# Loading expert 2's two weight matrices earlier in a kernel of linear attention and eight dense experts

## The chip, the cores and the metric

The kernel runs on one core of a Trainium2 chip. A core has five engines that run their own instruction streams in order: TensorE (PE in the profile, with its weight loads as PEld), VectorE (DVE), ScalarE (ACT), GpSimd (POOL) and SyncE (SP). They meet through semaphores. Transfers between HBM and the on-chip memory run on 16 DMA engines; SP and POOL issue them, and each of the two has a queue of its own (queue 1 for SP's, queue 0 for POOL's in the profile). The metric is device time in microseconds of one execution. Less is better.

## The reference

The input is a linear attention with 8 batches, 8 heads, 576 positions and head dimension 64, followed by eight experts that every token passes, with weights from a Sinkhorn routing:

```python
q_p, k_p = (phi(q), phi(k))                      # phi(x) = elu(x) + 1
kv = np.einsum('bhsd,bhse->bhde', k_p, v)
z = np.sum(k_p, axis=2)
x = num / den                                    # q_p @ kv over q_p . z, laid out as (4608, 512)

P = np.exp(x @ w_gate - max)                     # (4608, 8)
for _ in range(8):
    P /= P.sum(1, keepdims=True) + 1e-09
    P /= P.sum(0, keepdims=True) + 1e-09
    P *= N / E
for e in range(E):                               # E = 8 experts, each on all 4608 tokens
    h = np.maximum(x @ w1[e], 0.0)               # w1[e]: 512 x 1024
    out += P[:, e:e + 1] * (h @ w2[e])           # w2[e]: 1024 x 512
```

Each expert has two weight matrices of half a million elements. The kernel holds them as 16-bit floats, so each is 1 MB on the chip. All eight experts must be computed for all tokens, so the weights are read once per expert, and the work is almost all matrix multiplication.

## The kernel before, in words

**Tiling.** The 4608 tokens are nine groups of 512, which the code calls units (`g` = 0 to 8). The attention runs first, and expert 0 is woven into it. Experts 1 to 7 then run one after another over the nine groups, in the order `SUBS = [(0,), (1, 2), (3, 4), (5, 6), (7, 8)]`: one single unit and four double units of two groups each. A double unit takes two steps (`q` = 0 and 1), each for half of the hidden width of both groups. A step `n` is the first layer of one such half (`l1_half`) beside the second layer of a group whose hidden values are ready (`layer2`, lines 1065 to 1187).

**Seven products for eight.** Both layers multiply 2 by 2 blocks with seven products. This needs sums of the operands: of the tokens (in HBM as the tensors `xd`, seven blocks per unit, written once by `x_blocks`), of the weights (`combos`: four sums W of w1, line 1038, and four sums T of w2, line 1052), and of the hidden values (four sums S, line 1083). These sums run on VectorE.

**Names of the products.** In a step the first layer's products are `a1` to `a7` and `b1` to `b7` (lines 816 and after), the second layer's are `y1` to `y7` (line 1112). The order of TensorE is written out by hand, the same for every step, where A1, A5, A6, A3 and A2 are the next step's a1, a5, a6, a3 and a2:

```python
order = "y1 y5 y2 a7 y6 y3 a4 b1 b5 y7 b6 b3 b2 b7 A1 A5 y4 b4 A6 A3 A2".split()
```

**x blocks.** `x_load` (line 781) has SP load the seven blocks of a unit in the order 1, 5, 6, 3, 2, 7, 4, each 256 KB for a double unit. There are ten buffers for them (tiles `xs`), seven until the token tile is given up. A load waits until TensorE has read the block that lay in its buffer. From then on SP issues them in batches of seven while TensorE is in the `b` products of a unit's second step: blocks 3, 2, 7 and 4 of the next unit, whose first step is about to begin (its A1 and A5 are among TensorE's next products), and then blocks 1, 5 and 6 of the unit after that. The first loads behind the token tile also wait for the end of the routing (`P_sb`, line 586).

**Weights.** `load_w` (line 308) has POOL issue the loads. w1 takes two DMA issues of 512 KB, w2 of experts 1 to 7 takes one of 1024 KB. There are two buffers for each of w1 and w2, so expert 2's w1 goes into the buffer of expert 0's, and expert 2's w2 into that of expert 0's w2. POOL also adds two pieces of each group's second layer into the sums (line 1153, tiles `acc`), for experts 1 to 7, after ScalarE has scaled them (`st`, line 1150); the groups' tiles are acc_87 (group 0), acc_88 (group 1), acc_89, and so on.

**Planner.** No instruction is issued while `add(...)` runs. Each `add` hands a task to `_Plan`, with its engine, its assumed cost, the tasks that it depends on (`deps`) and its priority. `_Plan.run` then simulates the engines and emits the tasks in the order that comes out. For the front part, up to somewhat into expert 1's and expert 2's work, this order is not left to the simulation: the string `_FRONT` lists tasks by number and engine letter (g is POOL, m a DMA, s SP, n none), and `run` emits in exactly that order. It insists that each task is allowed at its place, which means that its `deps` are done and its buffer is free in the simulation. The hardware's semaphore waits come only from the data: who wrote or read a buffer last. `deps` of the planner set places in the order and add no wait of their own.

Tasks 1513, 1514 and 1515 are the buffer, the POOL issues and the DMA of expert 2's w1; tasks 1516, 1517 and 1518 are those of its w2.

Of the kernel before, what the change touches and what calls it, by code (L numbers as in the profile page):

```python
# [181 lines left out]
543d 1025p 986p 1029p 941a 937a 1026a 932d 944p 1030a 1031p 1027p 1028a 1033p 987a 544d 938p 545p 1034d 1035p 1037p 1036a 1038a 1032d  # L182
945d 1039p 1040a 546d 547d 933d 946p 1043p 1044a 1045p 1041p 1047p 1065p 548p 549d 550d 1046d 947a 988p 942p 1000n 1057s 1058m 943d
1059s 1060m 1048d 1042a 1061s 1062m 1063s 1064m 1066a 989p 996a 1147s 1148m 1149s 1150m 1067p 1068a 990p 1049p 1071p 1050a 1072a 1151s 1152m
728d 1005d 1006d 629a 1121d 991p 997a 992p 892a 1073p 994p 1122d 1007d 1069p 1123d 1074d 1070a 625a 1075p 627d 697a 993p 1076d 1077p
691d 1079p 1081p 664a 1080a 631d 1008d 1082a 1078a 995p 1085p 1086a 1087p 1083p 1089p 1093p 1095p 1124d 999d 1090d 1088d 998d 1091p 1084a
1094a 1513n 1099p 1096a 939d 1101p 1097p 1125p 1127p 1128d 695d 1092a 1100a 1129d 1126a 1130p 1131a 1103p 1135p 1138p 1104d 1105p 1107p 1136d
1098a 775d 1139d 1137d 662a 1109p 1141p 1106a 1108a 1113p 1516n 1153s 1154m 1155s 1156m 1110a 1115p 1114a 1133a 730a 1132g 1134g 1157s 1158m
1111p 1102d 1117p 1161p 1163p 1112a 1142d 1140d 1116d 1143d 1144p 1118d 1119p 1159s 1160m 1269s 1270m 1271s 1272m 1273s 1274m 1162a 1167p 1164a
658a 1120a 1169p 1168a 1165p 1146d 1145d 1189d 1190d 1193p 1195p 1194a 1198p 1171p 1203p 1166a 660a 1191d 1192d 1197d 726d 1196d 1201a 1202g  # L190
1199a 1206p 1172d 1173p 1174a 1175p 1176a 1177p 1178a 1205d 1204d 1209p 1181p 1182a 1183p 1179p 724d 1185p 1207d 1170d 1211d 1208d 1210d 1186d
1215p 693a 1217p 1212p 1187p 1243d 1200g 1514g 1515m 1244d 1214d 777d 1213d 1245d 774d 1246d 1180a 1216a 1221p 832a 1218a 1223p 1219p 1247p
1249p 1222a 1250d 1224d 1251d 1220a 1248a 1252p 1255a 1256g 951a 1188a 1225p 1226d 1184d 1257p 1259d 1260p 1258d 1519d 893d 1261d 1227p 1228a
1229p 1230a 1231p 1232a 833a 1263p 1235p 1237p 1275s 1276m 1233p 1236a 1239p 1253a 1264d 1520d 1521d 1265d 1277s 1278m 1279s 1280m 1281s 1282m
1283p 1391s 1392m 1393s 1394m 1285p 1266p 1240d 1234a 1284a 1238d 1241p 1289p 1286a 1291p 1287p 1395s 1396m 1242a 835a 1268d 1262d 1267d 1315p
1290a 1316a 1311d 1317p 1320p 1312d 1313d 1321a 1319d 1318d 1314d 1293p 1325p 1328p 776d 1294d 1295p 1288a 1327d 1330d 1326d 1329d 1297p 1299p
1331p 1296a 1298a 1303p 1292d 1300a 1305p 1301p 1332d 1365d 1333d 1304a 1307p 1337p 1339p 1334p 1366d 1302a 1517g 1518m 1254g 1308d 1309p 1323a
1338a 891a 1335d 1336d 1343p 1340a 1345p 1341p 1322g 950d 1369p 1371p 1344a 1342a 1370a 1374p 1347p 1379p 1346d 1522d 1367d 1373d 1368d 1372d
1382p 1377a 1310a 1378g 1324g 1348d 1349p 1351p 1352a 1380d 1306d 948d 1353p 1354a 1381d 1384d 1385p 1386d 1357p 1359p 1355p 1387d 1350a 1358a
1361p 1405p 1356a 1375a 1376g 1406a 1407p 1388p 1397s 1398m 1399s 1400m 1401s 1402m 1403s 1404m 1527s 1528m 1529s 1530m 1531s 1532m 1533s 1534m  # L200
# [21 lines left out]
def kernel(  # L222
# [85 lines left out]
    def load_w(ten, nm, pl, pieces, e, prio, deps=(), shape=None):  # L308
        g = S_.grp(pl)
        ts_ = []  # L310

        def f_al(_):
            g["tile"] = wpool.tile(shape, FP16, tag=nm, name=nm)
        tal = add(("none", 0.0), f_al, acq=[g], prio=prio, deps=deps)
        for part in pieces:
            def fn(_, part=part):
                for sl, off, ap in part:
                    nc.gpsimd.dma_start(out=g["tile"][sl], in_=AP(tensor=ten.tensor, offset=e * DM * F + off, ap=ap))
            gsw = [S_.grp(p_sw) for _ in part]
            ti = add(("pool", 0.8 * len(part)), fn, acq=gsw, use=[g, *gsw], prio=prio, deps=[tal, w_part.get(nm) if ts_ else None],  # L320
                     after=1.75)
            w_part[nm] = ti
            ts_.append(add(("dma", len(part) * (1.55 if len(part) * len(pieces) > 2 else 2.7)), lambda _: None, deps=[ti],
                           use=[g, *gsw], prio=prio, lat=2.15))
        return g, [ts_[0], ts_[-1]]

    def load_w1(e, parts=1, **kw):
        if parts > 1:
            return load_w(moe_w1, "w1", p_w1, [[((slice(64 * r, 64 * r + 64), slice(2 * i, 2 * i + 2)),
                                                 256 * F * r + 2 * PW * F * i, [[F, PW], [PW * F, 2], [1, F]]) for r in range(2)]  # L330
                                               for i in range(2)], e, shape=[P, NDT, F], **kw)
        return load_w(moe_w1, "w1", p_w1, [[((slice(64 * r, 64 * r + 64),), 256 * F * r, [[F, PW], [PW * F, NDT], [1, F]])
                                            for r in range(2)]], e, shape=[P, NDT, F], **kw)

    def load_w2(e, parts=1, **kw):
        n = NFT // parts
        return load_w(moe_w2, "w2", p_w2, [[((slice(None), slice(n * i, n * i + n)), n * i * P * DM,
                                             [[DM, P], [DM * P, n], [1, DM]])] for i in range(parts)], e,
                      shape=[P, NFT, DM], **kw)
# [284 lines left out]
    w_t = {0: load_w1(0, prio=-290.0, parts=2)}  # L624
# [151 lines left out]

    xst_of, xse_done, sx_users = {}, [], []

    n_load, first_x = [0], []

    def x_load(d, prio):
        gx = {}
# [135 lines left out]
    def l1_half(e, d, q, n, st):  # L918
        gw1, tw1 = w_t[e][:2]
        gW, tW = st["W"]  # L920
        un = NG + n
        dbl = len(SUBS[d]) == 2
        if q == 0:
            st["x"] = x_load(d, un)
            if n == 1:
                first_x.extend(t for _, t, _ in st["x"].values())
        gx = st["x"]
        r0, r1 = sorted((h_free.pop(0), h_free.pop(0)))
        slots = {0: (r0, r1)} if dbl else {0: (r0,), 1: (r1,)}
        if dbl:  # L930
            for s, r in enumerate((r0, r1)):
                st["h"].setdefault(SUBS[d][s], {})[q] = r
        else:
            st["h"][SUBS[d][0]] = {0: r0, 1: r1}
        blk = {i: gx[i][2] for i in ORD}
        for m in range(2):
            gi = 2 * q + m if dbl else m

            def F(i, p, gi=gi):
                return 2 * (gi if dbl else 2 * gi + p) + i - 1  # L940

            def A(i, j, F=F):
                return lambda p, c: gw1["tile"][:, 2 * (j - 1) + c, ts(F(i, p), P)]

            def W(i, gi=gi):
                return lambda p, c: gW["tile"][:, i - 1, c, gi if dbl else 2 * gi + p, :]

            def dst(fh, t, m=m):
                if dbl:
                    k = 2 * m + fh  # L950
                    a, b = 4 * r0 + k, 4 * r1 + k
                    return hb[:, a:b + 1:b - a, 256 * t:256 * t + 256]
                a = 4 * (r0, r1)[m] + fh
                return hb[:, a:a + 3:2, 256 * t:256 * t + 256]
            nm = {}
            rows = (r0, r1) if dbl else ((r0, r1)[m],)
            th = []
            pair(e, un, m, nm, 1 if dbl else 2, A, W, blk, dst, tw1, tW, [gw1, gW],
                 {i: ([gx[i][0]], [gx[i][1]]) for i in ORD}, th, [t for r in rows for t in h_users[r]],
                 n == 0, sx_users)  # L960
            for i, t in nm.items():
                pe_id[(n, f"{'ab'[m]}{i}")] = t
            pe_id[(n, "ab"[m] + "22")] = th[2]
            for s, g in enumerate(SUBS[d]):
                st["th"].setdefault(g, {0: [], 1: []})[q if dbl else m].extend(th)
# [288 lines left out]
    def second(n):  # L1254
        e, g = pend.pop(0)
        st = state[e]
        rows = st["h"][g]

        def H(j):
            return hb[:, 4 * rows[j]:4 * rows[j] + 4]  # L1260
        if not pend and n > len(steps):
            return last(g, NG + n, H, st["th"][g])
        own = layer2(e, g, NG + n - 1, H, st["th"][g], *st["T"], [])
        for j in range(2):
            h_users[rows[j]] = own
            h_free.append(rows[j])
        return None
    for n, (e, d, q) in enumerate(steps):
        if e not in state:
            if e >= 2:  # L1270
                w_t[e] = load_w1(e, prio=float(e), deps=w_t[e - 1][1][1:] + (first_x if e == 2 else [])) + load_w2(e, prio=float(e), deps=w_t[e - 1][3][1:])
            co = combos(e)
            state[e] = {"W": co[0:2], "T": co[2:4], "h": {}, "th": {}}
        l1_half(e, d, q, n, state[e])
        if n >= 2:
            second(n)
        if q == len(SUBS[d]) - 1:
            pend.extend((e, g) for g in SUBS[d])
# [10 lines left out]
    n = len(steps)  # L1289
# [38 lines left out]
```

## Time and profile before

| what | us |
|---|---|
| median of 3 runs | 961.14 |
| lowest and highest run | 959.94, 962.22 |
| the profiled execution, its own time | 963.2 |
| its span, from the first to the last instruction | 961.4 |
| TensorE busy in the span | 948.1 |
| VectorE busy in the span | 776.4 |
| ScalarE busy in the span | 582.8 |
| GpSimd busy in the span | 143.4 |

All places in time are microseconds from the span's start. Lines such as L1112 are lines of the kernel before. A row of the timeline gives the start, the length, the engine, the line, the operation, what it writes and reads, the shape and how many it stands for; in square brackets stands how long the engine had been idle ahead of it, and for what it waited. A matmul's row ends somewhat after the next one starts, since matmuls overlap; TensorE's pace is read from the starts. The granted clock is the share of its full clock that TensorE was given.

### The profile page before, as it was taken

Reading aid. Unit: us, or ns where it says so; the run is one execution under the profiler, and the core shown is the slowest. Engines: PE = TensorE matmul, PEld = TensorE weight load, DVE = VectorE, ACT = ScalarE, POOL = GpSimd, SP = SyncE. Lnnn points to the kernel's source line nnn. Section 1 sums busy time; section 2 is a strip of 40 time slices with the busy share of each in tenths; the row PEclk is TensorE's granted clock in tenths of the full one; section 3 lists DMA queues with packets and bytes.
Section 4 is the critical chain, followed back from the end, with each engine's and each line's share of the span. In section 5 each row is a group of like instructions: output and inputs, shape, how many; then the busy total and the mean of one; then the engine's idle time right before and its main releaser. Section 6 shows DMA issues by size and latency. Waiting matters only on the chain.

```text
span 961.4 us, 18327 instructions
## 1 busy us (share of the span) xinstructions
PE 948.1 (99%) x7008; PEld 652.8 (68%) x7008; DVE 776.4 (81%) x1500; ACT 582.8 (61%) x1033; POOL 143.4 (15%) x209
## 2 busy tenths in 40 slices
PE   8999999998999999999999999999999999999997
PEld 4565588665677666766667666766667666776665
DVE  7899999976888888878887888878887888877775
ACT  7899766765665555555555555555555555555551
POOL 6442000010111111111112111111112111111110
PEclk9999999998999999999999999999999999999999
DMA  9998863236226222642226422542226522215544
GB/s 242 255 247 190 198 159 105 78 91 151 77 68 131 83 77 78 148 105 76 71 72 141 105 78 77 125 97 74 73 74 154 119 78 77 72 45 164 165 133 132
DMA packets 81508, 112.65 MB, mean 117 GB/s; under 512 B 7436, under 2 KB 45196, under 8 KB 81420
## 3 DMA queue, kind: packets, MB, share of 16 engines
q1 hardware_dynamic: 56844, 75.65, 25.6%
q0 software_dynamic: 23856, 34.78, 19.3%
q8 instruction: 55, 0.90, 0.4%
q10 hardware_dynamic: 720, 1.05, 0.3%
q14 instruction: 33, 0.27, 0.1%
HBM read 119.69 MB, written 17.69 MB: 143 GB/s over the span
## 4 chain that ended last, share of the span: by engine, by line
PE 95%; DVE 2%; ACT 1%; DMA 1%; issue 0%; DVEq 0%
PE ye L1112 36%; PE hq L816 24%; PE R L816 12%; PE Zye L1112 6%; PE Zye L816 6%; PE ye L996 3%; PE hq L701 3%; PE yw L603 1%; PE kv_ps L427 1%; DMA xs<-xd 1%; PE att L484 1%; PE num_ps L484 1%; PE att L453 1%; PE hq L1208 0%; PE att L529 0%
## 5 line engine op out<-in xcount | busy, mean ns | idle before, releaser
L1143 DVE SCALAR_TENSOR_TENSOR acc<-ye,P_sb,acc 128x256 f32<-128x256 f32 x620 | 268.2, 479 | 133.0 <-PE ye L1112 131.0
L1112 PEld LDWEIGHTS <-S 128*128 128x128 f16 x1984 | 194.4, 98 | 47.0 <-DVE S L1083 0.2
L1112 PE MATMUL ye<-T,S 128*128 128x256 f16 x1488 | 193.7, 273 | 0.0
L1153 POOL TENSOR_TENSOR acc<-acc,st 128x256 f32<-128x256 f32 x124 | 88.2, 731 | 701.5 <-ACT st L1150 701.5
L1112 PEld LDWEIGHTS <-hb 128*128 128x128 f16 x1584 | 155.8, 98 | 44.1 <-issue 1.9
L816 PEld LDWEIGHTS <-W 128*128 128x128 f16 x1248 | 122.1, 98 | 88.1 <-DMA xs<-xd 2.3
L847 ACT ACTIVATE hb<-hq 128x512 f16<-128x512 f32 x134 | 80.0, 597 | 140.9 <-PE hq L816 135.6
L816 PE MATMUL R<-xs,W 128*128 128x512 f16 (+1 forms) x560 | 150.1, 358 | 1.8 <-DMA xs<-xd 1.8
L816 PE MATMUL hq<-xs,W 128*128 128x512 f16 (+1 forms) x560 | 150.1, 358 | 0.0
L816 PE MATMUL hq<-xs,w 128*128 128x512 f16 (+1 forms) x560 | 139.8, 358 | 0.0
L816 PEld LDWEIGHTS <-w 128*128 128x128 f16 x936 | 91.6, 98 | 61.2 <-issue 2.4
L844 ACT ACTIVATE hb<-Zye 128x512 f16<-128x512 f32 x134 | 80.1, 598 | 40.4 <-PE Zye L816 40.2
L1150 ACT ACTIVATE st<-Zye,P_sb 128x256 f32<-128x256 f32 x124 | 52.5, 471 | 78.4 <-PE Zye L1112 78.1
L850 DVE CUSTOM_DVE_ANT_0 hb<-hq,sx 128x512 f16<-128x512 f32 x126 | 86.6, 687 | 15.9 <-PE hq L816 15.7
L837 ACT COPY sx<-hq 128x512 f32<-128x512 f32 x126 | 73.5, 583 | 35.3 <-PE hq L816 35.3
L833 ACT COPY Zye<-hq 128x512 f32<-128x512 f32 x134 | 77.8, 580 | 21.1 <-PE hq L816 20.7
L850 DVE CUSTOM_DVE_ANT_0 hb<-R,sx 128x512 f16<-128x512 f32 x126 | 86.4, 685 | 4.9 <-ACT sx L837 3.8
L1083 DVE TENSOR_TENSOR S<-hb 128x1024 f16<-128x1024 f16 x124 | 84.9, 685 | 5.1 <-ACT hb L847 5.0
L816 PE MATMUL Zye<-xs,w 128*128 128x512 f16 (+1 forms) x280 | 75.4, 359 | 1.6 <-DMA xs<-xd 1.6
L841 ACT COPY sx<-R 128x512 f32<-128x512 f32 x126 | 74.4, 591 | 0.0
L1112 PE MATMUL ye<-w,hb 128*128 128x256 f16 x528 | 69.3, 275 | 0.6 <-DVE acc L1143 0.5
L1112 PE MATMUL Zye<-w,hb 128*128 128x256 f16 x528 | 69.3, 275 | 0.0
(120 smaller groups left out, 978.7 us busy)
## 6 DMA issues: line engine op xcount, KB each, us to landing
xs<-xd SPq DMA_DIRECT2D x196, 256.0 KB, 3.6
kin<-in_k_dram POOLq DMA_DIRECT2D x15, 576.0 KB, 7.5
w<-in_moe_w_dram POOLq DMA_DIRECT2D x16, 512.0 KB, 7.9
out_dram<-acc SPq DMA_DIRECT2D x63, 128.0 KB, 2.4
w<-in_moe_w_dram POOLq DMA_DIRECT2D x7, 1024.0 KB, 10.1
xs<-xd SPq DMA_DIRECT2D x49, 128.0 KB, 3.2
vv<-in_v_dram POOLq DMA_DIRECT2D x16, 288.0 KB, 7.3
hb<-in_q_dram POOLq DMA_DIRECT2D x15, 288.0 KB, 7.6
```

Of the source, the lines that this page charges most:

```text
L816: nc.tensor.matmul(dst_[:, p, :] if parts == 2 else dst_.rearrange("p a b -> p (a b)"), lhsT=lhs(p, c), rhs=blk[i](c), start=(first and p ...
L833: nc.scalar.copy(out=Zt[1], in_=gX["tile"])
L837: nc.scalar.copy(out=gs2["tile"], in_=gX["tile"])
L841: nc.scalar.copy(out=gs5["tile"], in_=gR["tile"])
L844: nc.scalar.activation(out=dst(0, 0), in_=Zt[1], func=AF.Relu)
L847: nc.scalar.activation(out=dst(1, 0), in_=gX["tile"], func=AF.Relu)
L850: nc.vector._custom_dve(TENSOR_ADD_SAT, out=out_, in0=ps, in1=sb, s0=3.0e38, s1=0.0)
L1083: nc.vector.tensor_tensor(out=Sx[:, i], in0=a0, in1=a1, op=op)
L1112: nc.tensor.matmul(bank(g_)[:, s, :], lhsT=lhs(s, kk), rhs=rhs(kk), start=(new and s == 0 and kk == 0), stop=(kk == 3), skip_group_check=True)
L1143: nc.vector.scalar_tensor_tensor(out=dst(), in0=bank(g_)[:, s, :], scalar=P_sb[:, gg, e:e + 1], in1=dst(), op0=ALU.mult, op1=ALU.add)
L1150: nc.scalar.mul(out=gst["tile"], in_=bank(g_)[:, s, :], mul=P_sb[:, gg, e:e + 1])
L1153: nc.gpsimd.tensor_tensor(out=dst(), in0=dst(), in1=gst["tile"], op=ALU.add)
```

## The change

The first load of expert 2 is planned behind the x blocks of step 1 (the first double unit of expert 1), as before, and its second load is now planned behind the x blocks of step 3 (the second double unit). For that a list `second_x` is kept beside `first_x`, and the w2 load of expert 2 has it among its `deps`. The places in `_FRONT` change with it: 1513 to 1515 move up to right behind the first double unit's x loads (task 1152 is the last of these), and 1516 to 1518 to right behind the second double unit's (task 1274). The numbers around them keep their order.

```diff
-728d 1005d 1006d 629a 1121d 991p 997a 992p 892a 1073p 994p ...
...
-1094a 1513n 1099p 1096a 939d 1101p 1097p 1125p 1127p ...
-1098a 775d 1139d 1137d 662a 1109p 1141p 1106a 1108a 1113p 1516n 1153s ...
...
-1215p 693a 1217p 1212p 1187p 1243d 1200g 1514g 1515m 1244d ...
...
-1331p 1296a 1298a 1303p 1292d 1300a 1305p 1301p ... 1302a 1517g 1518m 1254g 1308d 1309p 1323a
+1513n 1514g 1515m 728d 1005d 1006d 629a 1121d 991p 997a ...
...
+1158m 1111p 1102d ... 1159s 1160m 1269s 1270m 1271s 1272m 1273s 1274m 1516n 1517g
+1518m 1162a 1167p 1164a 658a 1120a ...
@@
-    n_load, first_x = [0], []
+    n_load, first_x, second_x = [0], [], []
@@
-            if n == 1:
-                first_x.extend(t for _, t, _ in st["x"].values())
+            if n in (1, 3):
+                (first_x if n == 1 else second_x).extend(t for _, t, _ in st["x"].values())
@@
-                w_t[e] = load_w1(e, prio=float(e), deps=w_t[e - 1][1][1:] + (first_x if e == 2 else [])) + load_w2(e, prio=float(e), deps=w_t[e - 1][3][1:])
+                w_t[e] = load_w1(e, prio=float(e), deps=w_t[e - 1][1][1:] + (first_x if e == 2 else [])) + load_w2(e, prio=float(e), deps=w_t[e - 1][3][1:] + (second_x if e == 2 else []))
```

In POOL's own stream the order was: the adds to acc_87 (two), to acc_88 (two), then expert 2's w1, one add to acc_89, expert 2's w2, the other add to acc_89. It is now: expert 2's w1, the two adds to acc_87, expert 2's w2, the two adds to acc_88, the two to acc_89. The streams of the other four engines are the same as before.

More of the change, by code (lines that the diff above doesn't have):

```diff
@@ L184 @@
 1059s 1060m 1048d 1042a 1061s 1062m 1063s 1064m 1066a 989p 996a 1147s 1148m 1149s 1150m 1067p 1068a 990p 1049p 1071p 1050a 1072a 1151s 1152m
-728d 1005d 1006d 629a 1121d 991p 997a 992p 892a 1073p 994p 1122d 1007d 1069p 1123d 1074d 1070a 625a 1075p 627d 697a 993p 1076d 1077p
-691d 1079p 1081p 664a 1080a 631d 1008d 1082a 1078a 995p 1085p 1086a 1087p 1083p 1089p 1093p 1095p 1124d 999d 1090d 1088d 998d 1091p 1084a
-1094a 1513n 1099p 1096a 939d 1101p 1097p 1125p 1127p 1128d 695d 1092a 1100a 1129d 1126a 1130p 1131a 1103p 1135p 1138p 1104d 1105p 1107p 1136d
@@ L188 @@
[L188 to L195, printed above, removed]
@@ L196 @@
-1290a 1316a 1311d 1317p 1320p 1312d 1313d 1321a 1319d 1318d 1314d 1293p 1325p 1328p 776d 1294d 1295p 1288a 1327d 1330d 1326d 1329d 1297p 1299p
-1331p 1296a 1298a 1303p 1292d 1300a 1305p 1301p 1332d 1365d 1333d 1304a 1307p 1337p 1339p 1334p 1366d 1302a 1517g 1518m 1254g 1308d 1309p 1323a
+1513n 1514g 1515m 728d 1005d 1006d 629a 1121d 991p 997a 992p 892a 1073p 994p 1122d 1007d 1069p 1123d 1074d 1070a 625a 1075p 627d 697a
+993p 1076d 1077p 691d 1079p 1081p 664a 1080a 631d 1008d 1082a 1078a 995p 1085p 1086a 1087p 1083p 1089p 1093p 1095p 1124d 999d 1090d 1088d
@@ new lines @@
+998d 1091p 1084a 1094a 1099p 1096a 939d 1101p 1097p 1125p 1127p 1128d 695d 1092a 1100a 1129d 1126a 1130p 1131a 1103p 1135p 1138p 1104d 1105p
+1107p 1136d 1098a 775d 1139d 1137d 662a 1109p 1141p 1106a 1108a 1113p 1153s 1154m 1155s 1156m 1110a 1115p 1114a 1133a 730a 1132g 1134g 1157s
+1158m 1111p 1102d 1117p 1161p 1163p 1112a 1142d 1140d 1116d 1143d 1144p 1118d 1119p 1159s 1160m 1269s 1270m 1271s 1272m 1273s 1274m 1516n 1517g
+1518m 1162a 1167p 1164a 658a 1120a 1169p 1168a 1165p 1146d 1145d 1189d 1190d 1193p 1195p 1194a 1198p 1171p 1203p 1166a 660a 1191d 1192d 1197d
@@ new lines @@
+726d 1196d 1201a 1202g 1199a 1206p 1172d 1173p 1174a 1175p 1176a 1177p 1178a 1205d 1204d 1209p 1181p 1182a 1183p 1179p 724d 1185p 1207d 1170d
+1211d 1208d 1210d 1186d 1215p 693a 1217p 1212p 1187p 1243d 1200g 1244d 1214d 777d 1213d 1245d 774d 1246d 1180a 1216a 1221p 832a 1218a 1223p
+1219p 1247p 1249p 1222a 1250d 1224d 1251d 1220a 1248a 1252p 1255a 1256g 951a 1188a 1225p 1226d 1184d 1257p 1259d 1260p 1258d 1519d 893d 1261d
+1227p 1228a 1229p 1230a 1231p 1232a 833a 1263p 1235p 1237p 1275s 1276m 1233p 1236a 1239p 1253a 1264d 1520d 1521d 1265d 1277s 1278m 1279s 1280m
@@ L198 @@
+1281s 1282m 1283p 1391s 1392m 1393s 1394m 1285p 1266p 1240d 1234a 1284a 1238d 1241p 1289p 1286a 1291p 1287p 1395s 1396m 1242a 835a 1268d 1262d
+1267d 1315p 1290a 1316a 1311d 1317p 1320p 1312d 1313d 1321a 1319d 1318d 1314d 1293p 1325p 1328p 776d 1294d 1295p 1288a 1327d 1330d 1326d 1329d
+1297p 1299p 1331p 1296a 1298a 1303p 1292d 1300a 1305p 1301p 1332d 1365d 1333d 1304a 1307p 1337p 1339p 1334p 1366d 1302a 1254g 1308d 1309p 1323a
 1338a 891a 1335d 1336d 1343p 1340a 1345p 1341p 1322g 950d 1369p 1371p 1344a 1342a 1370a 1374p 1347p 1379p 1346d 1522d 1367d 1373d 1368d 1372d
```

## The prediction

> **What bounds the kernel now.** I read the engines' shares first, then the chain of waits, then the one place after the start-up where that chain leaves TensorE for over 2 us in one piece, then each queue there.
>
> ```profile
> span 961.4 us, 18327 instructions
> PE 948.1 (99%) x7008; PEld 652.8 (68%) x7008; DVE 776.4 (81%) x1500; ACT 582.8 (61%) x1033; POOL 143.4 (15%) x209
> PE 95%; DVE 2%; ACT 1%; DMA 1%; issue 0%; DVEq 0%
> ```
>
> TensorE is busy 99% of the span and carries 95% of the chain. A change of queue order can gain only where TensorE stands still or runs slowly. The chain's 1% of DMA is one piece. In order of time (start, length, what):
>
> ```profile
> 223.13 1.75 PE ye L1112 x16
> 224.88 0.86 PE hq L816 x4
> 225.74 0.43 PE R L816 x2
> 226.18 0.03 PE ye L1112
> 226.21 9.17 DMA xs<-xd
> 235.42 1.01 PE Zye L816 x2
> 236.43 3.41 PE ye L1112 x16
> 239.84 1.71 PE Zye L1112 x8
> 241.99 1.75 PE ye L1112 x16
> ```
>
> An x block issued at 226.21 lands 9.17 us later. After it the same 16 matmuls take 3.41 us instead of 1.75. TensorE's timeline shows the two waits, and the windows (PE, PEld, DVE, ACT, POOL, then granted clock, DMA share, GB/s) the clock:
>
> ```profile
> 230.78 0.59 PE L816 MATMUL hq<-xs,W 128*128 128x512 f16 x2
> 233.16 0.60 PE L816 MATMUL R<-xs,W 128*128 128x512 f16 x2 [1.79 <-DMA xs<-xd]
> 235.42 1.01 PE L816 MATMUL Zye<-xs,w 128*128 128x512 f16 x2 [1.65 <-DMA xs<-xd]
> ...
> 231.30:234.58 3.28, 0.68 (x3) 0.21 (x3) 2.41 (x5) 1.36 (x3) 0.00 (x0) 1.00 1.13 287
> 234.58:241.40 6.82, 5.98 (x27) 3.93 (x27) 1.52 (x4) 0.57 (x1) 0.00 (x0) 0.50 0.38 141
> ```
>
> The waits are 1.79 + 1.65 = 3.44 us, and behind them the granted clock is 0.50 for 6.82 us. The DMA view of that stretch names the neighbour (queue 0 is POOL's, with w2 of expert 2, queue 1 SP's x blocks), and the issues have size and time to landing:
>
> ```profile
> q0 software_dynamic: 1039, 1.05, 66.4%
> q1 hardware_dynamic: 773, 1.42, 37.1%
> xs<-xd SPq DMA_DIRECT2D x7, 256.0 KB, 9.3
> ...
> w<-in_moe_w_dram POOLq DMA_DIRECT2D x1, 1024.0 KB, 12.4
> ```
>
> POOL issues this w2 at 224.05, right before SP's seven x blocks of 225.77 to 230.97. With no weight in flight the seven blocks issued from 201.37 land in 3.5 us (median). The loss as a whole: the first L1112 group of a TensorE period that reads S3 (y7) starts at 213.77, 226.01, 244.87 and 257.05; the steps are 12.24, 18.86 and 12.18, so the stall cost 18.86 - 12.21 = 6.65 us. The parts agree: 3.44 idle, and half of 5.98 busy us at half clock, 2.99, make 6.43.
>
> **The change, part by part.** In the built program the orders of PE, DVE, ACT and SP stay the same, instruction for instruction and wait for wait. Only POOL's differs: its three DMA issues for expert 2 move ahead of L1153 adds. Before: acc_87 twice, acc_88 twice, w1 (two issues of 512 KB), acc_89, w2 (one of 1024 KB), acc_89. After: w1, acc_87 twice, w2, acc_88 twice, acc_89 twice.
>
> *w1.* It now heads POOL's queue and waits for the last read of expert 0's w1, in whose buffer it goes. TensorE makes that read in the group hq<-sx,w at 170.59, which gives way at 171.03, so POOL issues near 171.2 instead of 212.49 (0.74 + 0.62 us of POOL, as before). Behind this wait stands the add at 199.00, which had waited 87.2 us for ACT: 28 us of cover. The pair landed 5.86 and 7.65 us after issue at 212, and 6.9 and 8.9 at 286.85; so it is in by 171.9 + 8.9 = 180.8 at the latest of these. SP's queue is moved past: its x issues of 157.66 and 181.25. Queue 1 carries nothing from 162.3 to 182.2. Nobody waited for w1 before (VectorE's W sums from 225.31 have no idle ahead of them). Cost 0, gain 0. If the cover fails, the x blocks of 181.25 are late (third rival).
>
> *w2.* It goes in behind the second acc_87 add (204.16 + 0.73), so at 204.9 instead of 224.05; expert 0's w2 is read until 191.2 (the L996 group at 190.16, 1.03 us), so its wait is over. Its 0.93 us end at 205.8; the acc_88 adds start at 211.13: nothing of POOL is late. Its first packets came 1.6 us after issue (225.7), so now about 206.5, and 10 to 12 us of landing make 215 to 217, long before the T sums at 260.85. SP's x issues that it now meets are 201.37, 201.81, 203.11, 203.54 (four blocks for the unit at hand) and 204.00, 204.47, 206.57 (the next unit's first three, read only from 228.6). The four land by 206.99, when w2 has hardly begun. They are read by A3 at 206.81, A2 at 207.24, a7 at 210.30 and a4 at 212.47. From below the cost is 0. From above, every block takes the stalled 9.31: 203.11 + 9.31 = 212.42 for a7, 2.1 us late; the first two have data flowing from 202.3, before POOL even issues. I take 0, since the last of the four has landed 0.5 us after w2's first packet.
>
> *The stretch that w2 leaves.* Blocks issued at 225.77 and 226.21 land like those of 201.37, in 3.4 to 3.7 us: 229.5 and 229.9. A3 follows on the group of 230.78 at 231.2 and A2 at 231.65, so 1.7 us of margin; both waits go, and with them the clock dip. Gain 6.65.
>
> *What is late next.* VectorE. It stood idle 6.14 us in the stall, and that rest goes. Its sums S1 to S3 end at 233.74; the next evacuation would be released at about 234.0 (y1 at 232.08, y5 0.87 later, 0.87 long), so no backlog is carried in. But before, that evacuation started 1.2 us into its (shifted) period, else 1.95 to 2.3: a head start of 0.75 is lost. From 241 to 258 VectorE has about 3 us of small idle pieces, the largest 0.79 at 249.40 and 0.54 at 258.12, which absorb it. Bounds: 0 and 0.75; I take 0.15, nearer to nothing, because those idles come before the tight stretch at 259 to 263.
>
> Sum: 6.65 - 0.15 = 6.5 us. Against the profiled execution: span 961.4 to 954.9, its own time 963.2 to 956.7. The median shown is 961.14 (959.94 to 962.22), 2.1 below that execution; taking the stall to be the same there, 954.6.
>
> **The rivals.**
>
> *The timed runs hold a smaller loss.* The profiled execution is 1 to 3.3 us above the timed ones, the size of the dip (2.99). If those mostly had the waits but no dip, only 3.44 goes: 957.7. For it: the spread. Against it: the profiled one lies 1.8 above its own span, so the median would allow a 959.3 span, still most of the stall. A rule of the Trainium skill bears on this (page "TensorE: Matmul & The Clock Gate", section "What's actually happening"): the clock halves after an idle window of about 3.4 us, and the windows run freely, whatever the kernel does. The trace agrees with the length, 6.82 us being two such windows; it has no single wait of 3.4, and whether two waits split by a matmul pair always trip it, one trace cannot say. By the rule some runs would save 3.4 and others about 6.5, as in this rival.
>
> *w2 hurts one period earlier.* a7 waits up to 2.1 us as priced: 954.6 + 2.1 = 956.7, and with a clock dip of 2.99 behind it 959.7. Against: the landings above.
>
> *Slower: w1 meets the first x blocks after routing.* The blocks of 181.25 and 181.63 are read at 185.76 and 187.06; the later two landed in 4.1 and 4.8, so margins are under 1 us. If w1 is still flowing at 182.2, they take 9.31: 190.56 - 185.76 = 4.8 us of wait, a dip of 2.99 to 3.4, and up to 0.5 for the next two: 8.3 to 8.7, of which 6.5 is paid back: 962.9 to 963.3. It decides once w1 lands later than 10.3 us after its second issue. Only the 12.9 of the third of three weights in a row at 110.89 is longer; the pairs show 7.7 and 8.9.
>
> That the change does nothing is excluded by POOL's order and the known release times.
>
> **How the numbers follow.** Stall gone: 0.74, at 954.6, its own range 953.5 to 956.0 (6.65 with nothing lost and 0.9 us for the median's own scatter; above, 0.75 for VectorE and some scatter). Smaller loss: 0.11, at 957.7. w2 earlier: 0.07, 956.7 to 959.7. w1 collides: 0.08, 962.9 to 963.3. The range 953.5 to 958.0 leaves out the last and part of the third. A measurement of this kernel tells some 0.2%, 1.9 us, from no change. Below 959.2 lie the first two and most of the third: faster 0.88; same 0.06 (the rest of the third and half of the fourth); slower 0.06.
>
> **What would show it.** Right: POOL's w1 issues near 171, w2 near 205; no TensorE wait for xs between 220 and 245; granted clock 1.00 throughout; y7 steps of about 12.2 all along; x blocks of about 226 landing in under 4 us. Wrong: a wait for xs at 185 to 189 or 207 to 213, a dip behind it, or VectorE named ahead of TensorE between 232 and 263. The forecast fails if the timed runs never had the dip, or if w1 takes over 10 us.

## The result, and the profile after

The median went from 961.05 us (959.94 to 962.22, 4 runs) to 956.43 us (955.83 to 957.13, 4 runs). The ratio is 0.9952, with a 95% interval of 0.9935 to 0.9969: faster by 4.6 us, between 3.0 and 6.2. The forecast was 954.6 with 953.5 to 958.0: the right direction, and 1.8 us too much of it. A later measurement gave 961.88 before and 956.53 after, ratio 0.9943 (0.9929 to 0.9958).

The page's first lines of the changed kernel, and its chain by engine:

```profile
span 954.1 us, 18327 instructions
PE 944.5 (99%) x7008; PEld 651.3 (68%) x7008; DVE 775.0 (81%) x1500; ACT 582.8 (61%) x1033; POOL 144.4 (15%) x209
PE 97%; ACT 1%; DVE 1%; issue 0%; DVEq 0%
```

The span of the profiled execution is 7.3 us shorter, and DMA has gone from the chain. The place where TensorE waited, in its timeline after:

```profile
230.19 0.59 PE L816 MATMUL hq<-xs,W 128*128 128x512 f16 x2
230.62 0.59 PE L816 MATMUL R<-xs,W 128*128 128x512 f16 x2
231.05 0.59 PE L816 MATMUL Zye<-xs,w 128*128 128x512 f16 x2
231.48 1.04 PE L1112 MATMUL ye<-w,hb 128*128 128x256 f16 x8
```

The same two windows as before (PE, PEld, DVE, ACT, POOL, then granted clock, DMA share, GB/s):

```profile
231.30:234.58 3.28, 3.28 (x29) 2.66 (x28) 2.96 (x6) 1.54 (x4) 0.00 (x0) 1.00 0.33 96
234.58:241.40 6.82, 6.82 (x47) 4.40 (x46) 6.34 (x13) 4.35 (x10) 0.95 (x1) 1.00 0.00 0
```

A3 and A2 follow their predecessors without a gap, and the granted clock is 1.00 where it was 0.50. POOL's timeline shows the moved issues:

```profile
172.19 1.25 POOL L318 DMA_DIRECT2D w<-in_moe_w_dram  x2 [60.94 <-issue]
198.41 0.73 POOL L1153 TENSOR_TENSOR acc<-acc,st 128x256 f32<-128x256 f32 x1 [24.98 <-ACT st L1150]
203.56 0.74 POOL L1153 TENSOR_TENSOR acc<-acc,st 128x256 f32<-128x256 f32 x1 [4.43 <-ACT st L1150]
204.24 0.92 POOL L318 DMA_DIRECT2D w<-in_moe_w_dram  x1
```

w1 goes out at 172.19 and w2 at 204.24. The x batch of 225.18 to 230.38 has no weight beside it, and its seven blocks land in 3.8 us (median; 9.3 before).

Where did 7.3 us of span come from? The group y7 that starts at 213.77 before starts at 213.18 after: 0.6 us lies ahead of everything the change touches (TensorE's group of 170.59 already starts at 170.01), so it is scatter between two executions. From there to the y7 three steps on it takes 43.28 us before (213.77 to 257.05) and 36.57 after (213.18 to 249.75): 6.71 us, the size of the stall. So the open question is why the medians differ by only 4.6 to 5.4.

### The profile page after: what moved, and what is told of

Same layout as the page of the kernel before. It is cut to its first block, busy times and chain, and to the rows that moved or that the text cites. A ratio compares the mean times of both kernels' runs of the same rounds, so it can differ in the third digit from the quotient of the medians.

```text
span 954.1 us, 18327 instructions
## 1 busy us (share of the span) xinstructions
PE 944.5 (99%) x7008; PEld 651.3 (68%) x7008; DVE 775.0 (81%) x1500; ACT 582.8 (61%) x1033; POOL 144.4 (15%) x209
## 4 chain that ended last, share of the span: by engine, by line
PE 97%; ACT 1%; DVE 1%; issue 0%; DVEq 0%
PE ye L1112 36%; PE hq L816 24%; PE R L816 12%; PE Zye L1112 6%; PE Zye L816 6%; PE ye L996 3%; PE hq L701 3%; PE kv_ps L427 1%; PE yw L603 1%; PE att L484 1%; PE num_ps L484 1%; PE att L453 1%; PE hq L1208 0%; PE att L529 0%; ACT rden L497 0%
## 5 line engine op out<-in xcount | busy, mean ns | idle before, releaser
L816 PEld LDWEIGHTS <-W 128*128 128x128 f16 x1248 | 122.1, 98 | 86.0
L816 PE MATMUL R<-xs,W 128*128 128x512 f16 (+1 forms) x560 | 150.0, 358 | 0.0
L816 PE MATMUL hq<-xs,W 128*128 128x512 f16 (+1 forms) x560 | 150.0, 358 | 0.0
L816 PE MATMUL hq<-xs,w 128*128 128x512 f16 (+1 forms) x560 | 139.7, 358 | 0.0
L816 PEld LDWEIGHTS <-w 128*128 128x128 f16 x936 | 91.6, 98 | 59.4 <-issue 0.5
L816 PE MATMUL Zye<-xs,w 128*128 128x512 f16 (+1 forms) x280 | 75.0, 358 | 0.0
```

Of the source, the lines that this page charges most:

```text
L816: nc.tensor.matmul(dst_[:, p, :] if parts == 2 else dst_.rearrange("p a b -> p (a b)"), lhsT=lhs(p, c), rhs=blk[i](c), start=(first and p ...
```

## The experiments

All start from the kernel before or the changed one. POOL's order alone is moved in the first four; the streams of the other four engines stay as they are in both. "Before" is the kernel before, measured beside each.

### Each half of the change alone

```diff
# e1_w1_only: against the kernel before
- 1094a 1513n 1099p ... 1200g 1514g 1515m 1244d ...
+ 1151s 1152m 1513n 1514g 1515m 728d ...          # w1 as in the changed kernel; w2's tasks where they were
```

> Half of the change: expert 2's w1 goes out near 171 as in the changed kernel, its w2 stays right before the x blocks of about 225. If the collision of w2 with those x blocks is the whole cause, w1's place is worth nothing: two waits for xs between 230 and 236 as before (together 3 to 4 us), and the time of the kernel before, 961 (960 to 962). If the gain came from POOL's three issues being out of the way in general, or from w1, about half of it shows: 958.5 to 959. If w1 at 171 does harm near the x blocks of 181, it is slower: 962 or more, with a wait for xs at 185 to 189.

Measured: 961.23 us (11 runs), before 961.46 (21 runs), ratio 1.0002 (0.9993 to 1.0011). The stall is there as ever, w2 at 224.29 and TensorE's timeline:

```profile
231.03 0.59 PE L816 MATMUL hq<-xs,W 128*128 128x512 f16 x2
233.54 0.60 PE L816 MATMUL R<-xs,W 128*128 128x512 f16 x2 [1.92 <-DMA xs<-xd]
235.21 0.60 PE L816 MATMUL Zye<-xs,w 128*128 128x512 f16 x2 [1.06 <-DMA xs<-xd]
```

Within 0.1%, w1's new place is worth nothing and does no harm.

```diff
# e2_w2_only: against the kernel before
- 1113p 1516n 1153s ... 1302a 1517g 1518m 1254g ...
+ 1273s 1274m 1516n 1517g 1518m 1162a ...          # w2 as in the changed kernel; w1's tasks where they were
```

> The other half: w2 goes out near 204.5 as in the changed kernel, w1 stays behind the acc_88 adds near 212, so that w1 now queues behind w2. If the collision of w2 with the x blocks of about 225 is the whole cause, all of the gain is here: 956.4 (955.8 to 957.2), no wait for xs between 220 and 245. w1, issued near 212 behind w2, should land by 225, when VectorE first reads it; if it does not, VectorE waits up to 2 us for it and part of the gain is lost (958). If the gain needs w1's move, the time stays near 961.

Measured: 956.02 us (955.83 to 956.11, 5 runs), ratio 0.9945 (0.9931 to 0.9958). No wait for xs anywhere. w1, issued at 211.99 behind w2, had landed when VectorE first read it at 224.80, and VectorE did not wait. All of the gain is w2's.

### w2 later instead of earlier

```diff
# e3_w2_later: against the kernel before
- ... 1302a 1517g 1518m 1254g 1308d ... 1322g ...
+ ... 1302a 1254g 1308d ... 1322g 1517g 1518m ...  # behind the first add to acc_90
```

> w1 as before (near 212), w2 not earlier but later than before: behind the first acc_90 add, near 236. It then flows between the x batches of about 225 and 249.5. If only the meeting with an x batch costs, being later is as good as being earlier: 956.4 (955.8 to 957.2) and no wait for xs; its landing near 248 is ahead of the first T sum near 253.6. If it is the earliness of w2 that helps (VectorE's T sums or POOL's adds relieved), the time stays near 961, or a wait of VectorE for w2 shows.

Measured: 956.03 us (955.87 to 956.28, 5 runs), ratio 0.9945 (0.9933 to 0.9958), w2 issued at 236.19, and no wait for xs. Twelve microseconds later is as good as twenty earlier. What counts is that w2 is not ahead of an x batch.

### The same collision, made elsewhere

```diff
# e4_w2_on_201: against the changed kernel (w1 as there, second_x taken out of w2's deps)
- 1132g 1134g ... 1273s 1274m 1516n 1517g 1518m 1162a ...
+ 1132g 1516n 1517g 1518m 1134g ... 1273s 1274m 1162a ...   # between the two adds to acc_87
```

> w1 as in the changed kernel, w2 earlier still: between the two acc_87 adds, near 199.2, which is 1.6 us ahead of the x batch of about 200.8, as it was 1.7 us ahead of that of 225.77 in the kernel before. If the meeting is the cause, the same stall comes one double unit earlier: two waits for xs of together 3 to 4 us near 206 to 211, a half-clock stretch behind them, and the time of the kernel before, 961 (959.5 to 962). If x blocks and w2 can share the engines at that place without harm, or if earlier is better, 956.4.

Measured: 962.02 us (959.55 to 962.53, 11 runs), ratio 1.0002 (0.9992 to 1.0012). w2 goes out at 199.47, the x batch from 201.17. TensorE's timeline:

```profile
206.22 0.59 PE L816 MATMUL hq<-xs,W 128*128 128x512 f16 x2
208.41 0.60 PE L816 MATMUL R<-xs,W 128*128 128x512 f16 x2 [1.60 <-DMA xs<-xd]
210.19 0.59 PE L816 MATMUL Zye<-xs,w 128*128 128x512 f16 x2 [1.17 <-DMA xs<-xd]
```

The window behind the waits (the granted clock is the third number from the end):

```profile
210.84:214.25 3.41, 3.41 (x19) 2.43 (x17) 0.20 (x1) 1.69 (x3) 0.00 (x0) 0.50 0.55 203
```

The stall stands two steps earlier than in e1 (206.22 against 231.03, 24.8 us), with its whole price. This shows the cause: w2 moved ahead of another batch makes the stall there, and w2 moved away on either side takes it off.

### How much of w2 has to be ahead

```diff
# e6_w2_half and e8_w2_quarter: against the kernel before, for expert 2's w2
- nc.gpsimd.dma_start(out=g["tile"][sl], in_=...)             # sl: all eight blocks, 1024 KB at 224
+ nc.gpsimd.dma_start(out=g["tile"][:, ...], in_=...)         # at 224: blocks 0:4 (e6, 512 KB) or 0:2 (e8, 256 KB)
+ ...                                                         # the rest in one issue behind the next add to acc_89, near 229
# e9_two_halves: both halves at 224, as two issues
```

> The kernel before, but w2 is cut in two issues of 512 KB: the first stays at 224, ahead of the x batch, the second goes behind the next acc_89 add, near 229, when the four urgent x blocks are issued. If the x blocks wait until the bytes of w2 that are ahead of them are through, half the bytes cost less than half: the wait of 3.9 us to the first x packet shrinks to about 2, block 3 lands by 231, no wait for xs or at most 0.7 us, no dip: 956.0 to 957. If any POOL load ahead of the batch makes x packets wait the same 3.9 us, the full 3 us of waits and the dip stay: 959 to 962.

> The kernel before, with 256 KB of w2 at 224 and the other 768 KB behind the next acc_89 add, near 229. With all of w2 ahead, the first x packet came 3.9 us after its issue and behind some 540 KB of w2; with half of it ahead, 3.1 us and behind 458 KB; with none, 1.0 us. If x packets wait for the bytes that are ahead of them, up to some 540 KB, the first x packet now comes 1.5 to 2.2 us after its issue, behind 200 to 256 KB, and no wait for xs shows. If what counts is that any POOL load is ahead, it comes 3 us or more after its issue again. Span near 954 in both cases.

> The kernel before, with w2 as two issues of 512 KB, both ahead of the x batch. If x packets wait for some 540 KB of whatever POOL has issued before them, however it is cut, the first x packet comes 3.5 to 4 us after its issue and the stall is as before: two waits for xs of 2.5 to 3.5 us together, 959 to 962.5. If a smaller issue is what let the half pass, the first x packet comes behind at most 460 KB, about 3 us after its issue, and the waits shrink to under 2 us: 957 to 959.

Measured: half ahead, 956.03 us (955.48 to 956.62, 5 runs; before 961.88), ratio 0.9940 (0.9926 to 0.9954), no wait for xs. A quarter ahead, a single run, span 954.9 and 956.74 us, no wait for xs. Two halves ahead, 958.62 us (957.65 to 963.69, 10 runs; before 961.54), ratio 0.9985 (0.9969 to 1.0001). Its runs fall in two groups, seven from 957.65 to 960.00 and three from 962.11 to 963.69. The profiled one is of the first group (958.82), with two waits (the lines of code inserted above make L816 L822 there):

```profile
232.90 0.61 PE L822 MATMUL R<-xs,W 128*128 128x512 f16 x2 [1.21 <-DMA xs<-xd]
234.16 0.59 PE L822 MATMUL Zye<-xs,w 128*128 128x512 f16 x2 [0.66 <-DMA xs<-xd]
```

What lies behind this is seen in the DMA packets between the issue of the first x block and its first packet. In the window of that wait (226.13 to 227.66 for the quarter, 226.09 to 229.80 for the two halves; queue, packets, MB, share of 16 engines) only POOL's queue has rows. The quarter ahead:

```profile
q0 software_dynamic: 198, 0.20, 90.4%
```

The two halves ahead:

```profile
q0 software_dynamic: 580, 0.58, 105.1%
```

| kernel | weight ahead of the batch, KB | issue of first x block to its first packet, us | weight moved by then, thousand bytes | waits of TensorE for xs, us |
|---|---|---|---|---|
| changed (batch of 225.18) | 0 | 0.9 | 0 | 0 |
| e8, a quarter | 256 | 1.5 | 237 | 0 |
| e6, half | 512 | 3.1 | 458 | 0 |
| before | 1024 | 3.8 | 553 | 1.79 + 1.65 |
| e1 | 1024 | 4.0 | 551 | 1.92 + 1.06 |
| e4 | 1024 | 3.9 | 537 | 1.60 + 1.17 |
| e9, two halves | 512 + 512 | 3.7 | 602 | 1.21 + 0.66 |

The x packets do not start beside w2's. They start when nearly all that is ahead of them has moved (237 of 262 thousand bytes, 458 of 524), or, where more is ahead, when 537 to 602 thousand bytes of it have; from then on the two queues flow together. In the four kernels with all of w2 ahead this takes 3.7 to 4.0 us; whether the bytes or the time set the limit, these runs do not tell, and a load issued ahead on SP's own queue was not tried. So the quarter came out as the first theory had it (1.5 us, 237 thousand bytes). The half started later than expected, at 3.1 us instead of about 2, but the x batch then has the engines nearly alone: 1 MB of it has begun by 231.4, against 234.9 with all of w2 ahead. For e9 this was the expectation of the first theory in the packets (3.5 to 4 us), but its profiled waits, 1.87 us together, and its median are those of the second, while three of its ten runs lie where the kernel before does. So neither theory holds for it as a whole.

One more thing differs between e9 and the three kernels that issue w2 in one piece: how long SP takes to issue the batch's second block, which A2 reads. The first row is of the kernel before, the second of the changed one:

```profile
226.21 1.20 SPq L793 DMA_DIRECT2D xs<-xd  x1
225.61 0.36 SPq L793 DMA_DIRECT2D xs<-xd  x1
```

It is 1.20, 1.04 and 0.99 us in before, e1 and e4, 0.49 in e9 and 0.36 in e6, e8 and the changed kernel. So behind a w2 in one piece SP's issuing was held up too, and not the packets alone. Why it was less so when w2 came as two issues, no run shows.

### w1 among the first batch behind the routing

```diff
# e7_w1_on_181: against the changed kernel, in load_w's fn
+ if nm == "w1" and e == 2:
+     nc.gpsimd.tensor_copy(out=gate[:, 0:1], in_=P_sb[:, 0, 0:1])    # POOL waits for the routing
```

> The changed kernel, with w1 held back until the routing's result is there, by a small copy of one column of it on POOL ahead of w1. w1 then goes out near 181.3, 0.6 us behind the first x block of 180.65 and among the other six. In the kernel before w2 went out 1.7 us ahead of such a batch, in the changed one 3.5 us behind one. If only x blocks that are issued behind the weight's packets suffer, the first two blocks land in time and the third and fourth (read at 186.9 and 188.2) come up to 2 us late: 956.0 to 958.5, with a dip in some runs. If any overlap costs a block the 9.3 us seen under w2, the waits add up to 4.8 us with a dip: 961 to 964, as the third rival had it.

Measured: 957.14 us (956.39 to 957.64, 5 runs; before 961.88), ratio 0.9952 (0.9939 to 0.9964), beside 956.53 for the changed kernel. w1 came out at 182.99, later than meant, between the fourth and the fifth x block, and its first packet 2.0 us after that. One wait, at a4 (L816 is L818 there, L996 is L998):

```profile
188.09 1.03 PE L998 MATMUL ye<-w,hb 128*128 128x512 f16 x4
190.11 1.04 PE L818 MATMUL hq<-xs,w 128*128 128x512 f16 x4 [0.99 <-DMA xs<-xd]
```

The block issued at 182.74, 0.25 us ahead of w1, landed in 7.3 us, where it takes 4.6 in the changed kernel; those ahead of it were in time. A block issued behind w2 took 9.2 to 9.3 us in place of 3.7 to 3.8. So overlap with a weight that was issued later cost a block 2.7 us, against some 5.5 for one that was issued ahead, and TensorE 1 us here.

### The changed kernel again, and the clock of every run

> The changed kernel again, beside the next two. 956.0 to 956.5, and every run's mean granted clock at 0.999 or 1.000, against runs of the kernel before at 1.000 (about 959.3), 0.998 (about 961.5) and 0.996 (about 962.3).

Measured: 956.53 us (955.09 to 957.80, 5 runs), ratio 0.9943. One of its five runs had a mean clock of 0.998 and 957.80; the expectation had all at 0.999 or 1.000.

Each timed run comes with its mean granted clock. 43 runs of the kernel before from three measurements, sorted by it:

| mean granted clock | runs of before | mean time, us | above 956.0 (e2, e3, e6) |
|---|---|---|---|
| 1.000 | 3 | 959.28 | 3.3 |
| 0.999 | 4 | 960.03 | 4.0 |
| 0.998 | 26 | 961.52 | 5.5 |
| 0.997 and 0.996 | 10 | 962.36 | 6.4 |

The profiles show what probably stands behind the classes. Half clock lasted 6.82 us in the profile of before (its mean clock is 0.996), and 3.41 us in those of e1 and e4 (0.998). In 3.41 us at half clock TensorE loses 1.7 us, which is 0.0018 of the span. The y7 steps give the whole stall: 17.13 us in e1 (226.26 to 243.39) and 16.92 in e4 (201.45 to 218.37), less 12.2, make 4.9 and 4.7, against 6.65 in before. So the two waits were followed by one stretch of half clock or by two, and the mean clocks suggest that most runs had one. The class of 1.000 lies 3.3 us above the kernels without the stall, about what the waits alone would cost; no profile of such a run, or of one of the four at 0.999, exists. The classes are not pure either: without the stall, five of the nine runs of the changed kernel have 0.999 (956.17 to 957.13) and one has 0.998 (957.80), so a mean clock does not say where the clock was lost.

## Why the prediction was right, and where its size was off

**The stall and its cause: right, and shown.** e1, e2, e3 and e4 tell it from w1, from being early as such, and from POOL's relief in general. How a load ahead holds the x blocks back stays open.

**w1 at no cost: right.** It went out at 172.19 where I had 171.2, landed in 5.6 and 7.6 us, and nothing waited. The extra microsecond (1.6 with the 0.6 that this execution is ahead) has no releaser in the profile and stays unexplained.

**w2 beside the batch of 201 at no cost: right.** The four urgent blocks were issued from 200.78 to 202.95, the last landed in 3.66 us, and w2's first packet came at 206.7.

**VectorE, 0.15 us: not needed.** In the profile 6.71 us came back where the stall was 6.65.

**The step that was off in size** is "taking the stall to be the same there": the 6.65 us of one execution were carried over to the median. That execution had the 6.82 us dip, the long one, and a mean clock of 0.996; 10 of 43 runs are at 0.996 or 0.997. Its own time of 963.2 lay above all of those shown. The most common class, 26 of 43, is that of the profiles with one stretch of 3.41, whose stall cost 4.7 to 4.9 us. What the runs showed in place of 6.5 is a mix by class: 3.3, 4.0, 5.5 and 6.4 us. This was the first rival, at 0.11. It had the spread as its evidence and named the mechanism, but it knew only "dip or none" and put its time, 957.7, at none; the truth lay between, at 956.4. That is 0.4 above the main story's own range of 953.5 to 956.0. The stated range took it in because it was drawn to 958.0 for the rivals, and there the forecast was lucky in its size.

On the rule of the Trainium skill named there (page "TensorE: Matmul & The Clock Gate", section "What's actually happening"): the stretches of 3.41 and 6.82 us are one and two of its windows, and that the same waits trip none, one or two would agree with windows that run whatever the kernel does. Where the rule asks for an idle window of about 3.4 us, the measurement differs: no wait here is longer than 1.92 us, and two waits of 2.8 to 3.4 together, split by a pair of matmuls, halved the clock in all three profiles that have them. The 1.87 of e9 and the 0.99 of e7 tripped nothing in their profiles.

**w2 one period earlier, the second rival, did not happen** in the changed kernel; e4 shows that it would have cost the whole gain, had w2 gone out one add earlier: 962.0, above the 956.7 to 959.7 of that rival, with the waits at A3 and A2 and not at a7.

**The third rival did not happen, and its price was not tested.** It gave every block that overlaps with w1 the 9.31 us of a block behind w2. In e7 the last two blocks issued ahead of w1 took 5.2 and 7.3 us, and TensorE waited 1 us, so not every overlap costs 8 us. But the rival's case, a w1 that is wholly ahead of that batch, was not tried.

A rule of the Trainium skill's page "DMA: Bandwidth & Descriptors" (section "Queues, rings and completion order") says that each DMA engine takes turns, packet by packet, between the queues that it has work for. The trace agrees once both flow: with w1 in e7, 0.57 MB of POOL's queue and 0.64 MB of SP's moved between 185 and 190. In before, e1 and e4 no such turns are seen for the first 3.8 to 4.0 us, in which some 0.54 MB of w2 moved and of the x blocks, already issued by SP, nothing. Whether these had reached the DMA engines by then, no trace shows.

None of the variants beats the changed kernel clearly: e2, e3 and e6 lie at 956.0 with ratios of 0.9940 to 0.9945, the changed kernel at 0.9943 and 0.9952, all within each other's intervals. From 120 us on its profile has one wait of TensorE, 0.5 us for VectorE, at 935.78, near the end.

## What to carry to other kernels

A load that nobody waits for can still set the end, by what is issued right behind it on another queue: look at what is in flight when a small urgent transfer goes out, and move the big one behind it or well away, earlier or later alike. If it cannot move, cutting it so that less is ahead may do: half was enough here. And a stall that is followed by a lower clock had no single price here; take it from the distribution of runs, with their granted clocks, and not from the one that was profiled.

## What was not expected of the hardware

Blocks issued on SP's queue 1.7 us behind a 1 MB load of POOL's moved nothing for 3.8 to 4.0 us, until 537 to 553 thousand bytes of that load had gone (three kernels), and only then flowed beside the rest. SP's issue of the second block took 0.99 to 1.20 us there, in place of 0.36. Issued ahead of the load they were in flight first and kept most of the rate: in the changed kernel the load's first packet came 2.5 us after its issue, when the urgent blocks had landed, the last of them in 3.7 us.
